# Turning the second product of pass B over to 512 columns of tokens, with block transposes on VectorE and stores in runs of 128 bytes

## The chip, the core and the metric

The kernel runs on one core of a Trainium2 chip. The metric is the device time of one execution in microseconds; 1086.42 us is the median of three runs before the change (1086.01 to 1088.9). TensorE (PE) multiplies, VectorE (DVE) and ScalarE (ACT) work elementwise, SyncE (SP) and GpSimd (POOL) start the DMAs. SBUF is the on-chip memory; PSUM holds TensorE's sums in eight banks, each of 128 partitions by 512 float32.

## The reference

Three stages, one after the other, all in float32, on 6016 tokens of 256 channels:

```
s = softmax over channels of (k normalised)^T (q normalised) / tau     # 256 x 256
x = v @ s                                                              # 6016 x 256
x = gelu(x @ moe_w_in) @ moe_w_out          # 256 -> 2048 -> 256   (pass A)
x = elu(x @ moe2_w_in) @ moe2_w_out         # 256 -> 2048 -> 256   (pass B)
```

gelu is h * sigmoid(1.702 h), elu is h for h > 0 and exp(h) - 1 otherwise. The softmax matrix is folded into moe_w_in, so that pass A starts from v.

## The kernel before

After a first phase that makes the 256 x 256 matrix, the kernel goes through two passes, A and B, of the same make. Each pass takes the tokens in six groups: five of 1024 tokens (8 slots of 128) and a last one of 896 (7 slots). Each group is computed in eight units p = 0 to 7, each for 256 of the 2048 hidden channels. A unit (kind, b, p) has two parts.

- The first product (`product`, L678) is a 2 x 2 block multiplication done with seven block products (the combinations of the operands are stored ahead), each of three matmuls of 512 columns, since every float32 operand is split into a high and a low part and high*high, high*low and low*high are summed. In the last group a matmul has 448 columns. The seven sums end in four quarters of the hidden values: C11, C12, C21 and C22 (hidden half i, token half X or Y).
- The nonlinearity takes each quarter through `s1` to `s4`: in pass B two ACT functions (L714, L715), two DVE operations (L725, L730), an ACT copy that is the high part (L737) and a DVE subtraction that is the low part (L741). L930 and L940 on DVE, L919 and L926 on ACT, make the sums that the block algorithm needs between its products.
- The second product (`second`) multiplies the hidden values by the second weight matrix and adds into PSUM banks 4 to 7 over all eight units of a group.

`step(t)` writes out the order by hand: it runs the first product and the nonlinearity of unit t, and between them, through `Q()`, the eight parts of the second product of unit t - 1. So TensorE's work in a step is product 1, Q, product 5, Q, products 6 and 2, two Qs, products 7 and 3, two Qs, product 4, two Qs. Every engine executes its instructions in the order in which they are written, and waits by semaphores. When unit t - 1 is the last of its group (p = 7), `step` calls `evacuate(before, 1)` after its sixth part (token half Y, banks 6 and 7), and `evacuate(before, 0)` early in the next step (token half X, banks 4 and 5). The next unit's second product, with p = 0, starts with half Y.

In pass A the second product is made with hidden channels in the rows of the stationary operand: a block of the weights (128 x 128) stays in TensorE and the hidden values of 512 tokens stream past it (L771), 24 matmuls per unit; the result has channels on the partitions and tokens along them. In pass B, 128 tokens of the hidden values are the stationary operand and 256 columns of weights stream past (L795), 48 matmuls per unit; the result has tokens on the partitions, as the output has. In pass B `evacuate` has four ACT copies per group from banks 4 to 7 to the tile `ob` (L825), and two DMAs on SP's queue, each partition writing four rows of the output, 4 KB in one run (L829).

During the first group of pass B, DVE and ACT also make the operands of the last group (`operands`, through `background(2)`, L964 in the listing: two pieces per step). At the end of each group SP's queue loads the seven operand tiles of the next one (L131).

Of the kernel before, what the change touches and what calls it, by code (L numbers as in the profile page):

```python
# [17 lines left out]
P = 128  # L18
# [4 lines left out]
def kernel(  # L23
# [40 lines left out]
    nc = tc.nc  # L64
    _, NT, C = q.shape
    DFF = w1.shape[1]
    KC = C // P
# [5 lines left out]
    HJ = SJ // 2  # L73
    groups = [(j, min(SJ, NJ - j)) for j in range(0, NJ, SJ)]
    NG = len(groups)
# [8 lines left out]
    ov = out.rearrange("(p j) c -> p j c", j=NJ)  # L84
# [13 lines left out]
    bank = [ps.tile([P, BANK], F32, name=f"b{i}") for i in range(8)]  # L98
# [290 lines left out]
    def full_tile(kind, b):  # L389
        full[kind, b] = stg.tile([P, KC, 2 * BANK], F32, tag="vt", name="vt")  # L390
        return full[kind, b]
# [111 lines left out]
    with tc.manual_schedule():  # L503
        make_identity(nc, ident)

        with ExitStack() as st:
# [24 lines left out]
            for i, m in enumerate(CHUNKS):  # L531
                t = wts.tile([P, 2, MM, C], F32, tag=f"wA{1 + i % 3}", name="qk")
# [6 lines left out]
                if i == 4:  # L539
                    nc.sync.dma_start(  # L540
                        out=tau_sb,
                        in_=tau.rearrange("(o a) -> o a", o=1).to_broadcast([P, 1]),
# [39 lines left out]
            for i in range(2):  # L582
                for c in range(KC):
                    x = i * KC + c
# [29 lines left out]
            e = ph1.tile([P, KC, C], F32, name="e")  # L614
            mn = ph1.tile([P, KC], F32, name="mn")
            sm = ph1.tile([P, KC], F32, name="sm")
            for c in range(KC):
                nc.vector.scalar_tensor_tensor(
                    out=e[:, c, :], in0=s_ps[c][:, :C], scalar=rk[:, c:c + 1], in1=rq,
# [125 lines left out]
        def fresh(key):  # L745

            if key in opened:
                return False
            opened.add(key)
            return True  # L750

        def acc_A(d, k):
            return 4 + 2 * k + d

        def second(u):

            kind, b, p = u
            n = wid[b]
            m = groups[b][1]
            w = w_second[kind, p]  # L760
            X, Y = 0, 1
            parts_ = []
            if kind == "A":
                seq = [(0, X), (0, Y), (1, Y), (1, X)] if p else [(0, Y), (0, X), (1, Y), (1, X)]
                for f, k in seq:
                    for d in range(KC):
                        def part(f=f, k=k, d=d):
                            g = g_t[kind, b, p, f]
                            a = acc_A(d, k)
                            for i, (wi, gi) in enumerate(((0, 0), (0, 1), (1, 0))):  # L770
                                nc.tensor.matmul(  # L771
                                    bank[a][:, :n],
                                    w[:, f, wi, d * P:(d + 1) * P],
                                    g[:, gi, k * n:(k + 1) * n],
                                    start=fresh((kind, b, a)),
                                    stop=(p == NP - 1 and f == 1 and i == 2),
                                    skip_group_check=True,
                                )
                        parts_.append(part)
            else:  # L780
                lowX = list(range(HJ)) if n == BANK else list(range(n // P))
                hiX = list(range(len(lowX), m))
                lowY = list(range(HJ, m))
                hiY = list(range(HJ))
                seq = [(0, lowX), (0, hiX), (1, lowY), (1, hiY)] if p else \
                    [(0, lowY), (0, hiY), (1, lowY), (1, hiY)]
                for f, slots in seq:
                    cut = (len(slots) + 1) // 2
                    for ss in (slots[:cut], slots[cut:]):
                        def part(f=f, ss=ss):  # L790
                            g = g_t[kind, b, p, f]
                            for s in ss:
                                a = 4 + s // 2
                                for gi, wi in ((0, 0), (0, 1), (1, 0)):
                                    nc.tensor.matmul(  # L795
                                        bank[a][:, s % 2 * C:(s % 2 + 1) * C],
                                        g[:, gi, s * P:(s + 1) * P],
                                        w[:, f, wi, :],
                                        start=fresh((kind, b, a)),
                                        stop=(p == NP - 1 and f == 1 and gi == 1),  # L800
                                        skip_group_check=True,
                                    )
                        parts_.append(part)
            return parts_
# [3 lines left out]
        def evacuate(u, k):  # L808

            kind, b, _ = u  # L810
            n = wid[b]
            j, m = groups[b]
            if kind == "A":
                t = full.get(("B", b))
                if t is None:
                    t = full_tile("B", b)
                for d in range(KC):
                    nc.scalar.copy(t[:, d, k * n:(k + 1) * n], bank[acc_A(d, k)][:, :n])
                return
            if b not in out_t:  # L820
                out_t[b] = tp.tile([P, SJ, C], F32, tag="ob", name="ob")
            o = out_t[b]
            for a in (0, 1) if k == 0 else (2, 3):
                w = min(2, m - 2 * a)
                nc.scalar.copy(  # L825
                    o[:, 2 * a:2 * a + w, :].rearrange("p s d -> p (s d)"), bank[4 + a][:, :w * C]
                )
            lo, hi = (0, HJ) if k == 0 else (HJ, m)
            nc.sync.dma_start(out=ov[:, j + lo:j + hi, :], in_=o[:, lo:hi, :])  # L829


# [24 lines left out]
        def step(t):  # L856
            nonlocal roles, late
            u = units[t] if t < len(units) else None
            before = units[t - 1] if t else None
            qs = second(before) if before else []  # L860
            last = before and before[2] == NP - 1

            def Q(n=1):
                for _ in range(n):
                    if not qs:
                        if not t:
                            spare(4)
                        return
                    qs.pop(0)()
                    if last and len(qs) == 2:  # L870
                        evacuate(before, 1)
                    if last and not qs:
                        if u is None:
                            evacuate(before, 0)
                        else:
                            late_out.append(lambda: evacuate(before, 0))
# [146 lines left out]
        for t in range(len(units) + 1):  # L1023
            u = units[t] if t < len(units) else None
            if u:
                kind, b, p = u
# [62 lines left out]
```

## Time and profile before

| | |
|---|---|
| median of three runs | 1086.42 us (1086.01 to 1088.9) |
| profiled execution | 1085.72 us, of which the span of the trace is 1084.0 us |
| granted TensorE clock, mean | 0.996 of full speed |
| TensorE matmul busy | 1056.2 us (97%), 5768 matmuls |
| VectorE busy | 830.6 us (77%) |
| ScalarE busy | 769.2 us (71%) |
| pass B, 40 slices view | TensorE 9 tenths or more, VectorE 8, DMA mostly 0 or 1 |

Busy TensorE time counts matmuls that overlap at their ends, so it says little of how much faster the work could go; what one step takes is read from the starts of successive matmuls in the timeline. The table's shares are means over a kernel with a first phase of some 65 us, a pass A and a pass B.

### The profile page before, as it was taken

What the parts mean: (1) busy time and instruction counts of PE and PEld (TensorE: products, weight loads), DVE (VectorE), ACT (ScalarE), POOL (GpSimd) and SP (SyncE); (2) the same over time, 40 slices, a digit from 0 to 9 for tenths busy, and PEclk for the clock granted to TensorE, in tenths of its full rate; (3) what the DMA queues carried; (4) which work ended last, traced back from release to release, by engine and by line L of the source; (5) the groups of instructions that cost most, each with busy time, mean ns of one, the idle gap of its engine ahead of it and who ended that gap; (6) DMA issues with size and microseconds to landing.
All of it is one profiled execution on the core that took longest, in us unless ns stands there. A gap on an engine that the chain in (4) does not pass through costs nothing.

```text
span 1084.0 us, 15552 instructions
## 1 busy us (share of the span) xinstructions
PE 1056.2 (97%) x5768; PEld 922.9 (85%) x5768; DVE 830.6 (77%) x1346; ACT 769.2 (71%) x1443; POOL 72.3 (7%) x126
## 2 busy tenths in 40 slices
PE   7978989999999999999899999999999999999998
PEld 6867868888888888888798998998998999999997
DVE  5888786677777776666437998888888888888886
ACT  5768767667767777676457777767677776767775
POOL 0000011012112221120000100000000000000000
PEclk9999999999999999999999999999999999999999
DMA  9913255358558557445745114004004003003100
GB/s 330 355 47 94 58 201 186 111 193 281 178 196 277 183 202 258 140 150 202 287 168 208 69 62 165 2 1 175 1 1 156 20 2 136 39 1 120 40 1 35
DMA packets 82845, 144.42 MB, mean 133 GB/s; under 512 B 46864, under 2 KB 51056, under 8 KB 82256
## 3 DMA queue, kind: packets, MB, share of 16 engines
q1 hardware_dynamic: 66624, 84.04, 23.2%
q0 software_dynamic: 16144, 59.38, 14.9%
q8 instruction: 45, 0.74, 0.3%
q14 instruction: 32, 0.26, 0.1%
HBM read 86.25 MB, written 57.15 MB: 132 GB/s over the span
## 4 chain that ended last, share of the span: by engine, by line
PE 63%; issue 15%; DVE 8%; ACT 6%; DMA 4%; POOL 3%; SPq 0%; POOLq 0%; DVEq 0%; ACTq 0%
PE b L678 29%; PE b L795 21%; PE b L771 11%; DMA qk<-in_k_dram 2%; DVE g L741 1%; DVE ee L725 1%; PE b L565 1%; DVE gg L730 1%; ACT ee L714 1%; ACT th L715 1%; DMA xdB<-xt 1%; POOL xdA L431 1%; POOL xdB L431 1%; PE b L474 1%; ACT g L737 1%
## 5 line engine op out<-in xcount | busy, mean ns | idle before, releaser
L795 PEld LDWEIGHTS b<-wBB,g 128*128 128x128 f32 x2256 | 301.7, 190 | 21.2 <-DVE g L741 2.3
L795 PE MATMUL b<-wBB,g 128*128 128x256 f32 x2256 | 309.0, 282 | 1.3 <-DVE g L741 1.0
L771 PE MATMUL b<-g,wBA 128*128 128x512 f32 (+1 forms) x1152 | 296.7, 386 | 1.7 <-DVE g L741 1.7
L678 PE MATMUL b<-xA,wAA 128*128 128x512 f32 (+1 forms) x1008 | 266.7, 388 | 9.7 <-ACT b L919 4.5
L678 PE MATMUL b<-xB,wAB 128*128 128x512 f32 (+1 forms) x1008 | 267.9, 389 | 0.2 <-DVE b L930 0.2
L771 PEld LDWEIGHTS b<-g,wBA 128*128 128x128 f32 x1152 | 216.9, 188 | 42.8 <-DVE g L741 2.2
L678 PEld LDWEIGHTS b<-xA,wAA 128*128 128x128 f32 x1008 | 188.0, 188 | 50.4 <-ACT b L919 8.4
L678 PEld LDWEIGHTS b<-xB,wAB 128*128 128x128 f32 x1008 | 174.2, 189 | 20.9 <-DVE b L930 0.4
L737 ACT CAST g<-gg 128x512 fp32r<-128x512 f32 (+1 forms) x192 | 118.3, 616 | 93.3 <-DVE gg L730 93.2
L725 DVE SCALAR_TENSOR_TENSOR ee<-ee,th 128x512 f32<-128x512 f32 (+1 forms) x192 | 129.9, 677 | 32.0 <-ACT th L715 31.9
L930 DVE TENSOR_TENSOR b<-b,s 128x512 f32<-128x512 f32 (+1 forms) x96 | 66.0, 687 | 111.7 <-PE b L678 105.3
L708 ACT ACTIVATE g<-b 128x512 fp32r<-128x512 f32 (+1 forms) x144 | 85.0, 590 | 86.8 <-PE b L678 86.3
L741 DVE TENSOR_TENSOR g<-gf,g 128x512 fp32r<-128x512 f32 (+1 forms) x192 | 128.4, 674 | 16.0 <-ACT gf L709 15.8
L741 DVE TENSOR_TENSOR g<-gg,g 128x512 fp32r<-128x512 f32 (+1 forms) x192 | 129.5, 675 | 11.0 <-ACT g L737 6.5
L714 ACT ACTIVATE ee<-b 128x512 f32<-128x512 f32 (+1 forms) x144 | 84.5, 587 | 34.8 <-PE b L678 34.6
L730 DVE SCALAR_TENSOR_TENSOR gg<-b,ee 128x512 f32<-128x512 f32 (+1 forms) x144 | 98.0, 680 | 4.9
L709 ACT ACTIVATE gf<-b 128x512 f32<-128x512 f32 (+1 forms) x144 | 84.4, 586 | 2.9 <-DVE g L741 2.5
L715 ACT ACTIVATE th<-b 128x512 f32<-128x512 f32 (+1 forms) x144 | 84.0, 583 | 0.0
L940 DVE TENSOR_TENSOR c<-b,s 128x512 f32<-128x512 f32 (+1 forms) x96 | 64.7, 674 | 23.1 <-PE b L678 22.9
L926 ACT COPY s<-b 128x512 f32<-128x512 f32 (+1 forms) x96 | 56.3, 586 | 27.0 <-PE b L678 26.1
L919 ACT COPY b<-b 128x512 f32<-128x512 f32 (+1 forms) x96 | 56.2, 585 | 16.9 <-PE b L678 16.8
L565 PE MATMUL b<-qk 128*128 128x256 f32 x188 | 44.1, 392 | 7.1 <-DMA qk<-in_k_dram 7.1
(98 smaller groups left out, 745.7 us busy)
## 6 DMA issues: line engine op xcount, KB each, us to landing
xdB<-xt POOLq DMA_DIRECT2D x35, 512.0 KB, 3.6
xB<-xdB SPq DMA_DIRECT2D x35, 512.0 KB, 5.3
xdA<-xt POOLq DMA_DIRECT2D x28, 512.0 KB, 3.2
xA<-xdA SPq DMA_DIRECT2D x28, 512.0 KB, 6.2
wAB<-w3d SPq DMA_DIRECT2D x4, 1792.0 KB, 7.9
out_dram<-ob SPq DMA_DIRECT2D x11, 512.0 KB, 2.6
qk<-in_q_dram SPq DMA_DIRECT2D x9, 512.0 KB, 6.4
qk<-in_k_dram SPq DMA_DIRECT2D x9, 512.0 KB, 7.3
```

Source lines behind the costliest of these rows:

```text
L678: nc.tensor.matmul(dst[:, :n], w[:, wi, p % 2, WOP[i], :], x[:, xi, :n], start=(start and k == 0), stop=(k == 2), skip_group_check=True,)
L708: nc.scalar.activation(self.sl(ik)[0], h, AF.Gelu_apprx_sigmoid)
L709: nc.scalar.activation(t[:, :n], h, AF.Gelu_apprx_sigmoid)
L714: nc.scalar.activation(e[:, :n], h, AF.Exp)
L715: nc.scalar.activation(t[:, :n], h, AF.Tanh, scale=0.5)
L725: nc.vector.scalar_tensor_tensor(out=e[:, :n], in0=e[:, :n], scalar=1.0, in1=t[:, :n], op0=ALU.add, op1=ALU.mult,)
L730: nc.vector.scalar_tensor_tensor(out=g[:, :n], in0=h, scalar=0.0, in1=e[:, :n], op0=ALU.max, op1=ALU.min)
L737: nc.scalar.copy(self.sl(ik)[0], self.tmp[ik][:, :self.n])
L741: nc.vector.tensor_sub(lo, self.tmp.pop(ik)[:, :self.n], hi.bitcast(F32))
L771: nc.tensor.matmul(bank[a][:, :n], w[:, f, wi, d * P:(d + 1) * P], g[:, gi, k * n:(k + 1) * n], start=fresh((kind, b, a)), stop=(p == NP - ...
L795: nc.tensor.matmul(bank[a][:, s % 2 * C:(s % 2 + 1) * C], g[:, gi, s * P:(s + 1) * P], w[:, f, wi, :], start=fresh((kind, b, a)), stop=(p ...
L930: nc.vector.tensor_add(bank[c][:, :n], bank[b][:, :n], s5[:, :n])
```

## The change

The second product of pass B takes the form that it has in pass A: the weights are the stationary operand and 512 columns of tokens stream past (in the changed kernel L776), 24 matmuls per unit in place of 48. This holds for the five groups of 1024 tokens; the last group keeps the rows (`by_rows`). The sums then lie with channels on the partitions. `evacuate` turns them on VectorE: per half of a group two transposes of 128 x 512 from PSUM to `ob` (L834), each of which transposes every square block of 32 x 32 by itself. The blocks are then not yet at their place across partitions, which the stores put right: 16 DMAs per half, each of 32 partitions with 8 runs of 32 floats, 128 bytes (L843). ScalarE's copies of these groups are gone.

```diff
+        def by_rows(kind, b):
+            return kind == "B" and b == NG - 1
...
-            if kind == "A":
+            if not by_rows(kind, b):
                 seq = [(0, X), (0, Y), (1, Y), (1, X)] if p else [(0, Y), (0, X), (1, Y), (1, X)]
...
+            lo, hi = (0, HJ) if k == 0 else (HJ, m)
+            if not by_rows(kind, b):
+                o = o.rearrange("p s (d x e) -> p s d x e", d=KC, e=32)
+                for d in range(KC):
+                    nc.vector.transpose(
+                        o[:, lo:hi, d, :, :].rearrange("p s x e -> p s (x e)"),
+                        bank[acc_A(d, k)][:, :n].rearrange("p (s t) -> p s t", t=P),
+                    )
+                dst = ov[:, j + lo:j + hi, :].rearrange(
+                    "(x p) s (d y e) -> x y p (s d) e", p=32, d=KC, e=32
+                )
+                for x in range(P // 32):
+                    for y in range(P // 32):
+                        nc.sync.dma_start(
+                            out=dst[x, y],
+                            in_=o[32 * y:32 * (y + 1), lo:hi, :, x, :].rearrange(
+                                "p s d e -> p (s d) e"
+                            ),
+                        )
+                return
             for a in (0, 1) if k == 0 else (2, 3):
```

On TensorE the order of the trains stays the same and each train of the second product changes its shape. The rows are the first products and parts of the step after the group change from the fourth to the fifth group of pass B (b_79 and the like are PSUM banks: 76 is bank 0, 80 to 83 are banks 4 to 7; xB and wAB belong to the first product). Before:

```order
L678 MATMUL b_79<-xB,wAB 128x512 x3
L795 MATMUL b_82<-wBB,g 128x256 x6
L678 MATMUL b_76<-xB,wAB 128x512 x3
L795 MATMUL b_83<-wBB,g 128x256 x6
L678 MATMUL b_78<-xB,wAB 128x512 x3
```

And in the changed kernel:

```order
L678 MATMUL b_79<-xB,wAB 128x512 x3
L776 MATMUL b_82<-g,wBB 128x512 x3
L678 MATMUL b_76<-xB,wAB 128x512 x3
L776 MATMUL b_83<-g,wBB 128x512 x3
L678 MATMUL b_78<-xB,wAB 128x512 x3
```

Nothing has moved against its neighbours; six matmuls of 256 columns have become three of 512.

On VectorE four transposes come into the order at each group change. The rows run from the low part of C11 in the first step of the fifth group to L930 of the next step (`ee`, `th`, `gg` are temporaries of the nonlinearity, `g` its result). Before:

```order
L741 TENSOR_TENSOR g<-gg,g 128x512
L725 SCALAR_TENSOR_TENSOR ee<-ee,th 128x512
L730 SCALAR_TENSOR_TENSOR gg<-b_78,ee 128x512
L741 TENSOR_TENSOR g<-gg,g 128x512
L725 SCALAR_TENSOR_TENSOR ee<-ee,th 128x512
L730 SCALAR_TENSOR_TENSOR gg<-c_8732,ee 128x512
L725 SCALAR_TENSOR_TENSOR ee<-ee,th 128x512
L730 SCALAR_TENSOR_TENSOR gg<-b_77,ee 128x512
L741 TENSOR_TENSOR g<-gg,g 128x512
L930 TENSOR_TENSOR b_77<-b_78,s_8848 128x512
```

And in the changed kernel, where L930 is L956:

```order
L834 STREAM_TRANSPOSE ob<-b_82 128x4x128
L834 STREAM_TRANSPOSE ob<-b_83 128x4x128
L725 SCALAR_TENSOR_TENSOR ee<-ee,th 128x512
L730 SCALAR_TENSOR_TENSOR gg<-b_78,ee 128x512
L741 TENSOR_TENSOR g<-gg,g 128x512
L725 SCALAR_TENSOR_TENSOR ee<-ee,th 128x512
L730 SCALAR_TENSOR_TENSOR gg<-c_8078,ee 128x512
L834 STREAM_TRANSPOSE ob<-b_80 128x4x128
L834 STREAM_TRANSPOSE ob<-b_81 128x4x128
L725 SCALAR_TENSOR_TENSOR ee<-ee,th 128x512
L730 SCALAR_TENSOR_TENSOR gg<-b_77,ee 128x512
L741 TENSOR_TENSOR g<-gg,g 128x512
```

The transposes of banks 6 and 7 stand behind the low part of C11 and ahead of the first operation on C12; those of banks 4 and 5 stand behind the operations on C22 and ahead of those on C21. The rest keeps its order. On SP's queue the 32 stores of a group stand where its two stores stood: behind the operand loads of the next group and ahead of those of the one after that.

## Rows read from the trace of the kernel before

**Rows 1.** The page's first part: busy time and share of each engine.
```profile
PE 1056.2 (97%) x5768; PEld 922.9 (85%) x5768; DVE 830.6 (77%) x1346; ACT 769.2 (71%) x1443; POOL 72.3 (7%) x126
```
**Rows 2.** Timeline, TensorE, pass A: start, duration (us), engine, line, operation, count.
```profile
381.30 0.84 PE L678 MATMUL b<-xA,wAA 128*128 128x512 f32 x3
...
384.02 1.52 PE L678 MATMUL b<-xA,wAA 128*128 128x512 f32 x6
385.38 1.52 PE L771 MATMUL b<-g,wBA 128*128 128x512 f32 x6
...
391.50 0.84 PE L678 MATMUL b<-xA,wAA 128*128 128x512 f32 x3
```
**Rows 3.** Timeline, TensorE, within a step of pass B.
```profile
703.48 1.55 PE L678 MATMUL b<-xB,wAB 128*128 128x512 f32 x6
...
704.87 1.60 PE L795 MATMUL b<-wBB,g 128*128 128x256 f32 x12
...
706.30 1.55 PE L678 MATMUL b<-xB,wAB 128*128 128x512 f32 x6
```
**Rows 4.** Timeline, a group change of pass B; brackets: idle before, releaser.
```profile
742.99 0.86 PE L678 MATMUL b<-xB,wAB 128*128 128x512 f32 x3
...
746.75 0.70 DVE L930 TENSOR_TENSOR b<-b,s 128x512 f32<-128x512 f32 x1 [0.46 <-PE b L678]
...
747.19 1.60 PE L795 MATMUL b<-wBB,g 128*128 128x256 f32 x12
...
748.51 0.69 DVE L725 SCALAR_TENSOR_TENSOR ee<-ee,th 128x512 f32<-128x512 f32 x1 [0.47 <-ACT th L715]
...
749.24 0.69 DVE L730 SCALAR_TENSOR_TENSOR gg<-b,ee 128x512 f32<-128x512 f32 x1
...
750.62 0.69 DVE L741 TENSOR_TENSOR g<-gg,g 128x512 fp32r<-128x512 f32 x1
...
751.46 1.08 ACT L825 COPY ob<-b 128x512 f32<-128x512 f32 x2
751.60 0.69 DVE L725 SCALAR_TENSOR_TENSOR ee<-ee,th 128x512 f32<-128x512 f32 x1 [0.29 <-ACT th L715]
...
753.57 0.86 PE L678 MATMUL b<-xB,wAB 128*128 128x512 f32 x3
...
754.12 0.69 DVE L741 TENSOR_TENSOR g<-gg,g 128x512 fp32r<-128x512 f32 x1 [1.10 <-ACT g L737]
...
754.73 0.69 DVE L725 SCALAR_TENSOR_TENSOR ee<-ee,th 128x512 f32<-128x512 f32 x1
...
754.87 0.74 PE L795 MATMUL b<-wBB,g 128*128 128x256 f32 x4 [0.21 <-DVE g L741]
...
755.45 0.69 DVE L730 SCALAR_TENSOR_TENSOR gg<-c,ee 128x512 f32<-128x512 f32 x1
```
**Rows 5.** The same view where TensorE's next but one step starts.
```profile
764.62 0.86 PE L678 MATMUL b<-xB,wAB 128*128 128x512 f32 x3
```
**Rows 6.** Chain of waits in the first group of pass B: start, duration, what.
```profile
587.67 0.60 ACT ee L714
588.27 0.50 ACT th L715
...
631.66 1.65 PE b L678 x6
```
**Rows 7.** VectorE by line and form: count, busy us, mean ns, idle before.
```profile
L930 DVE TENSOR_TENSOR b<-b,s 128x512 f32<-128x512 f32 x80 | 55.9, 698 | 87.0 <-PE b L678 82.5 <-ACT xt L425 3.4 <-ACT wBA L245 1.0
L207 DVE TENSOR_SCALAR bits<-raw 128x512 int32<-128x512 int32 x32 | 14.2, 444 | 0.0
L378 DVE STREAM_TRANSPOSE vt<-v_raw 128x512 f32<-128x512 f32 x18 | 12.5, 702 | 10.8 <-DMA v_raw<-in_v_dram 10.8
L523 DVE TENSOR_TENSOR sq<-sq 128x1024 f32<-128x1024 f32 x9 | 11.0, 1224 | 6.8 <-ACT sq L549 6.8
```
**Rows 8.** Timeline, SyncE's queue in pass A: one half of a group of v.
```profile
202.71 8.46 SPq L371 DMA_DIRECT2D v_raw<-in_v_dram  x16
```

More of the change, by code (lines that the diff above doesn't have):

```diff
@@ L827, in evacuate @@
                 )
-            lo, hi = (0, HJ) if k == 0 else (HJ, m)
             nc.sync.dma_start(out=ov[:, j + lo:j + hi, :], in_=o[:, lo:hi, :])
```

## The prediction, made before the changed kernel ran

> **What bounds the kernel now.** I read the page's busy shares first: TensorE is busy for 97% of the span, VectorE for 77%, ScalarE for 71% [rows 1]. Busy time of overlapping matmuls says little about what a cheaper form would give, so the timelines of the two passes come next, read by starts. In pass A six matmuls of 512 columns take 385.38 - 384.02 = 1.36 us, whichever product they belong to, and a whole step of 15 trains of three lasts 391.50 - 381.30 = 10.20 us, which is 15 x 0.68 [rows 2]. In pass B six of 512 take 704.87 - 703.48 = 1.39 us, the twelve of 256 that stand in for six of 512 take 706.30 - 704.87 = 1.43 us [rows 3], and a whole step lasts 753.57 - 742.99 = 10.58 us [rows 4]. So in both passes TensorE sets the pace of an ordinary step, and the same column count costs 0.38 us more in the row form of B: 8 trains at 0.035 us more, the rest in the first products between them.
>
> VectorE is the engine next to the bound. In an ordinary step of B it stands still three times, 0.46 us for TensorE, 0.47 us for ScalarE behind TensorE, and 0.29 us for ScalarE behind VectorE itself [rows 4]. The last of these goes round within VectorE and ScalarE and does not shrink with TensorE; so VectorE's own round is about 10.58 - 0.46 - 0.47 = 9.65 us, still under 10.20.
>
> There are two kinds of place where that reserve is not there. One is the first group of B, in which the operands of the last group are made beside the steps: there the chain of waits, from 587.67 us until TensorE's product at 631.66 us, runs through ScalarE and VectorE with no TensorE piece in it [rows 6]. The other is the step after each group change: it lasts 764.62 - 753.57 = 11.05 us, 0.47 us too long [rows 4, 5], since TensorE waits for the low part of C12, which VectorE makes at 754.12 us behind ScalarE's two copies to `ob`.
>
> **The change, part by part.**
>
> *The matmuls.* Forty second products are turned over (five groups of eight units). The order of trains is then that of pass A, with the same shapes and the same sizes of operands; I take pass A's 10.20 us per step. 40 x 0.38 = 15.2 us off TensorE's path (the last of them runs beside products of 448 columns and is counted like the others). From below, the gain is nothing, if the spacing stays at 10.58; from above I see no row under 10.20.
>
> *The first group.* Of these 15.2 us, those between 587.67 and 631.66 us do not come: the chain there does not touch TensorE, and its VectorE and ScalarE work is unchanged. That stretch is four steps and a train pair, of which TensorE would save 4 x 0.38 + 0.07 = 1.6 us. The wait for VectorE at its end grows by that. 15.2 - 1.6 = 13.6.
>
> *The transposes.* Per group four of 128 x 512, from PSUM, on VectorE; they replace four copies on ScalarE, where time is not short. The trace has no block transpose from PSUM. The nearest rows: a transpose of the same size from SBUF takes 0.702 us, an addition that reads PSUM takes 0.698 us [rows 7]. I take 0.70. Bounds: from below the fastest operation on 512 elements, 0.444 us; from above one over 1024 elements, 1.224 us, which would be the price if a transpose from PSUM went at half rate [rows 7].
>
> [...]
>
> What queues behind them: VectorE executes in order, so the first pair (banks 6 and 7) delays C12, the second pair (banks 4 and 5) delays C21 and L930. I go through one group change with zero at product 1 of its first step, TensorE at 0.68 us a train. VectorE's L725 for C11 comes at 748.51 - 742.99 = 5.52 us before; it hangs on product 2, which ends at 6 x 0.68 = 4.08 instead of 747.19 - 742.99 = 4.20, so 5.40. L741 for C11 follows 750.62 - 748.51 = 2.11 later: 7.51. One operation comes 0.61 after an independent one (754.73 - 754.12), and 0.72 after one whose result it reads (755.45 - 754.73) [rows 4]. First transpose 8.12, second 8.75 (its bank is finished at 12 x 0.68 = 8.16 and a little), L725 for C12 at 9.38, L730 at 10.10, L741 1.38 later (750.62 - 749.24) at 11.48, finished at 12.17, at TensorE some 0.06 later (754.87 - 754.12 - 0.69). TensorE wants it with the second matmul of the next step's first part, at 10.20 + 0.68 + 0.23 = 11.11. It waits 1.12 us.
>
> Going on: L725 for C22 12.09, L730 12.81, transposes 13.42 and 14.05, L725 for C21 14.68, L730 15.40, L741 16.01, L930 16.61 to 17.31. Product 7 overwrites what L930 reads; TensorE wants to start it at 10.20 + 8 x 0.68 + 1.12 = 16.76 and gets it at 17.35: another 0.59 us. Nothing later is short: banks 4 and 5 are free at 14.75, wanted at 15.4, and VectorE gains about 0.55 us on TensorE per step from here. So each change costs 1.71 us in place of 0.47, 1.24 more; five of them 6.2 us.
>
> *ScalarE.* Four copies per group go. They hide in no bound except at the change, where the copies made L737 late; there VectorE's queue is later still, so their going gives nothing more.
>
> *The stores.* Per group 32 DMAs in place of 2, all on SP's queue. Sixteen loads of the same cut (32 partitions, 128-byte runs) hold SP for 8.46 us [rows 8], so the stores hold it for some 17 us. Behind them stand the operand loads of the group after, six to seven steps or over 60 us later; `ob` is next written after 80 us; the last group, whose stores end the kernel, is not changed. I count nothing. The cover would be gone only if 32 stores took over four times as long as 32 loads.
>
> [...] No row of before shows such a store; the loads of the same cut are in rows 8.
>
> *Sum.* 15.2 - 1.6 - 6.2 = 7.4 us less. The profiled execution of 1085.72 us would be 1078.3; it lies 0.7 us under the median, so the median goes from 1086.42 to 1079.0 us, 0.7% faster.
>
> **The rivals.**
>
> *A. The group change costs no more than before.* VectorE's three stops per step hold 1.22 us, and if the transposes fell into them, only the first group would be lost: 1086.42 - 13.6 = 1072.8 us. Against it: the transposes must wait for the sums in banks 6 and 7, and by then VectorE's next operand is almost there.
>
> *B. A transpose from PSUM is slow, and the result is slower than before.* All four of a change stand in VectorE's order ahead of L930, so each tenth of a microsecond more costs 0.4 us per change and 2.0 us in all. At 1.224 us: 20 x 0.52 = 10.4 us more, 1089.4 us. It decides from 0.70 + 7.4 / 20 = 1.07 us per transpose on. For it: a transpose turns 32 columns into 32 partitions, and none from PSUM was seen. Against it: neither transposes nor operands in PSUM are dear in rows 7. At 0.444 us it would go the other way, to 1073.9.
>
> *C. No gain per step.* Either three matmuls of 512 do not go at 0.68 us here, or VectorE's round is really above 10.20 us and becomes the bound; then steps stay at 10.58. The change at that pace: C12's low part at 12.35 us against 11.52 wanted, then L930 late by 0.43 more, 1.26 us against 0.47; five times 0.8 is 4 us lost: 1090.4 us. For it: VectorE's margin per step is only 0.55 us. Against it: pass A runs the same trains, and two of the three stops are for TensorE.
>
> *D. The stores hold up the loads.* If 32 stores took five times 17 us, 85 us, the next group's operands would come some 15 us late or more, four times: about 1140 us. Nothing in the trace speaks for it but the missing row.
>
> **How the numbers follow.** Forecast 0.67, A 0.11, B 0.10, C 0.09, D 0.03. The forecast's own range is 1076 to 1083 (0.16 us either way on a transpose is 3 us, and 0.3 us on a change 1.5 us). The range of 1072 to 1086 leaves out the slow end of B, C and D, and a little of A. A measurement of this kernel can tell a difference of about 0.3%, 3.3 us; faster means under 1083.2. The forecast is that for nearly all of its chance, A for all, B for its fast end: 0.79. B between 0.9 and 1.2 us a transpose, and a forecast that lost a few more microseconds, fall within: 0.08. The rest of B, C and D: 0.13.
>
> **What would show it.** Starts of products in an ordinary step of B 10.20 us apart from the second group on, and no shorter in the first group between its second and fifth step. L834 at about 0.70 us. The step after a change near 11.9 us, with TensorE waiting once for L741 and once for L956. SP finished with the 32 stores long before the next operand loads. The prediction is wrong if steps stay above 10.3 us, if L834 takes over 0.9 us, or if a change costs under 0.8 us or over 2.5 us.

## The result and the profile after

The changed kernel takes 1078.53 us (median of four runs, 1078.05 to 1079.06) against 1086.32 for the kernel before in the same comparison, a ratio of 0.9919 with a 95% interval of 0.9905 to 0.9933: 7.8 us, 0.8% less. The prediction said 1079.0 us. The profiled execution took 1078.05 us, with a span of 1076.3 us.

The page's first part of the changed kernel answers [rows 1]:

```profile
PE 1047.0 (97%) x4808; PEld 873.5 (81%) x4808; DVE 840.7 (78%) x1366; ACT 759.6 (71%) x1423; POOL 72.1 (7%) x126
```

TensorE has 960 matmuls fewer, VectorE 20 operations more, ScalarE 20 fewer, and the shares are as good as unchanged: from this line nobody could tell that the kernel is faster. The steps tell it. The timeline of the changed kernel around the group change that [rows 4, 5] show for before:

```profile
740.00 0.84 PE L678 MATMUL b<-xB,wAB 128*128 128x512 f32 x3
...
744.08 1.52 PE L776 MATMUL b<-g,wBB 128*128 128x512 f32 x6
...
745.44 1.52 PE L678 MATMUL b<-xB,wAB 128*128 128x512 f32 x6
...
747.50 0.69 DVE L741 TENSOR_TENSOR g<-gg,g 128x512 fp32r<-128x512 f32 x1
...
748.11 1.31 DVE L834 STREAM_TRANSPOSE ob<-b 128x512 f32<-128x512 f32 x2
...
749.34 0.65 DVE L725 SCALAR_TENSOR_TENSOR ee<-ee,th 128x512 f32<-128x512 f32 x1
749.45 16.39 SPq L843 DMA_DIRECT2D out_dram<-ob  x32
...
750.20 0.84 PE L678 MATMUL b<-xB,wAB 128*128 128x512 f32 x3
...
751.40 0.69 DVE L741 TENSOR_TENSOR g<-gg,g 128x512 fp32r<-128x512 f32 x1 [0.68 <-ACT g L737]
751.43 0.49 PE L776 MATMUL b<-g,wBB 128*128 128x512 f32 x1 [0.39 <-ACT g L737]
...
752.15 0.74 PE L776 MATMUL b<-g,wBB 128*128 128x512 f32 x2 [0.23 <-DVE g L741]
...
752.73 0.87 PE L678 MATMUL b<-xB,wAB 128*128 128x512 f32 x3
...
753.34 1.31 DVE L834 STREAM_TRANSPOSE ob<-b 128x512 f32<-128x512 f32 x2
...
756.47 0.69 DVE L956 TENSOR_TENSOR b<-b,s 128x512 f32<-128x512 f32 x1
...
757.21 1.65 PE L678 MATMUL b<-xB,wAB 128*128 128x512 f32 x6 [0.19 <-DVE b L956]
...
758.71 1.52 PE L776 MATMUL b<-g,wBB 128*128 128x512 f32 x6
...
762.11 0.84 PE L678 MATMUL b<-xB,wAB 128*128 128x512 f32 x3
```

Read it by starts. An ordinary step lasts 750.20 - 740.00 = 10.20 us, where it was 10.58; six matmuls of the second product take 745.44 - 744.08 = 1.36 us, where twelve narrow ones took 1.43 [rows 3]. The step after the change lasts 762.11 - 750.20 = 11.91 us, where it was 11.05 [rows 4, 5]. In it TensorE waits where its three brackets stand. Two of them are at the first part of the second product: it waits for the high part of C12 (L737, at 751.43), and one matmul later for the low part (L741, at 752.15). The third is for L956, before product 7. In front of the first two stands the first pair of L834 on VectorE, in front of the third both pairs. L741 of C11 (747.50) and L956 (756.47) keep their places around them; the listing of the changed kernel's order ahead begins behind the one and ends in front of the other.

The first group of B gained nothing from the start of step 2 to that of step 6 (steps are counted from 0). Before:

```profile
593.86 0.86 PE L678 MATMUL b<-xB,wAB 128*128 128x512 f32 x3
...
631.66 1.65 PE L678 MATMUL b<-xB,wAB 128*128 128x512 f32 x6 [0.23 <-DVE b L930]
...
636.72 0.86 PE L678 MATMUL b<-xB,wAB 128*128 128x512 f32 x3
```

And in the changed kernel:

```profile
593.31 0.84 PE L678 MATMUL b<-xB,wAB 128*128 128x512 f32 x3
...
620.23 1.66 PE L678 MATMUL b<-xB,wAB 128*128 128x512 f32 x6 [0.34 <-DVE b L956]
...
631.30 1.65 PE L678 MATMUL b<-xB,wAB 128*128 128x512 f32 x6 [0.44 <-DVE b L956]
...
636.19 0.84 PE L678 MATMUL b<-xB,wAB 128*128 128x512 f32 x3
```

These four steps last 42.86 us before and 42.88 after; what TensorE would have saved it now waits for VectorE, at 620.23 and at 631.30, where before only the second wait was there, and shorter.

For all that the change touches, take pass B from product 1 of its step 1 to that of its last step: 1064.27 - 582.25 = 482.02 us before and 1056.88 - 582.00 = 474.88 after, 7.14 us less. The granted clock was 1.00 in both stretches, so the difference is not the clock's. This measure is better than the whole time for what follows, since the part ahead of pass B, the same in all kernels here, ended between 582.0 and 586.8 us in the profiled executions.

### The profile page after: what moved, and what is told of

Same layout as the page of the kernel before. It is cut to its first block, busy times and chain, and to the rows that moved or that the text cites. A ratio compares the mean times of both kernels' runs of the same rounds, so it can differ in the third digit from the quotient of the medians.

```text
span 1076.3 us, 13797 instructions
## 1 busy us (share of the span) xinstructions
PE 1047.0 (97%) x4808; PEld 873.5 (81%) x4808; DVE 840.7 (78%) x1366; ACT 759.6 (71%) x1423; POOL 72.1 (7%) x126
## 4 chain that ended last, share of the span: by engine, by line
PE 61%; issue 16%; DVE 12%; ACT 5%; POOL 3%; DMA 3%; SPq 0%; DVEq 0%; POOLq 0%; ACTq 0%
PE b L678 28%; PE b L776 28%; PE b L800 4%; DVE gg L730 2%; DVE ee L725 2%; DVE sq L523 1%; DVE g L741 1%; DMA qk<-in_k_dram 1%; DVE ob L834 1%; DMA xdB<-xt 1%; PE b L474 1%; POOL xdA L431 1%; ACT g L737 1%; POOL xdB L431 1%; DVE b L956 1%
## 5 line engine op out<-in xcount | busy, mean ns | idle before, releaser
L776 PE MATMUL b<-g,wBA 128*128 128x512 f32 (+1 forms) x1152 | 296.6, 386 | 1.7 <-DVE g L741 1.7
L776 PE MATMUL b<-g,wBB 128*128 128x512 f32 x960 | 252.3, 390 | 2.9 <-ACT g L737 1.8
L776 PEld LDWEIGHTS b<-g,wBA 128*128 128x128 f32 x1152 | 216.9, 188 | 42.9 <-DVE g L741 2.2
L678 PEld LDWEIGHTS b<-xB,wAB 128*128 128x128 f32 x1008 | 186.3, 188 | 40.0 <-DVE b L956 4.6
L776 PEld LDWEIGHTS b<-g,wBB 128*128 128x128 f32 x960 | 179.8, 188 | 43.4 <-ACT g L737 3.9
L737 ACT CAST g<-gg 128x512 fp32r<-128x512 f32 (+1 forms) x192 | 117.9, 614 | 114.2 <-DVE gg L730 110.1
L956 DVE TENSOR_TENSOR b<-b,s 128x512 f32<-128x512 f32 (+1 forms) x96 | 65.9, 687 | 100.9 <-PE b L678 93.5
L741 DVE TENSOR_TENSOR g<-gf,g 128x512 fp32r<-128x512 f32 (+1 forms) x192 | 128.5, 674 | 16.0 <-ACT gf L709 15.8
L741 DVE TENSOR_TENSOR g<-gg,g 128x512 fp32r<-128x512 f32 (+1 forms) x192 | 129.4, 674 | 8.9 <-ACT g L737 4.4
```

What stands on the lines that cost most here:

```text
L678: nc.tensor.matmul(dst[:, :n], w[:, wi, p % 2, WOP[i], :], x[:, xi, :n], start=(start and k == 0), stop=(k == 2), skip_group_check=True,)
L737: nc.scalar.copy(self.sl(ik)[0], self.tmp[ik][:, :self.n])
L741: nc.vector.tensor_sub(lo, self.tmp.pop(ik)[:, :self.n], hi.bitcast(F32))
L776: nc.tensor.matmul(bank[a][:, :n], w[:, f, wi, d * P:(d + 1) * P], g[:, gi, k * n:(k + 1) * n], start=fresh((kind, b, a)), stop=(p == NP - ...
L956: nc.vector.tensor_add(bank[c][:, :n], bank[b][:, :n], s5[:, :n])
```

## The experiments

The theory: the gain is the step of 10.20 us in place of 10.58, and the price is VectorE's order at the group change and in the first group. The rivals: the price comes from the quicker matmuls or the first use of C12 by themselves; the gain comes in part from ScalarE's freed copies; the stores disturb something.

**The transposes taken away (e1_act_copy).**

```diff
-                    nc.vector.transpose(
+                    nc.scalar.copy(
                         o[:, lo:hi, d, :, :].rearrange("p s x e -> p s (x e)"),
```

> The changed kernel with the 20 block transposes on VectorE replaced by 20 plain copies on ScalarE at the same places in the program; the blocks stay unturned, so the layout of the output is left out. Theory (VectorE's order at the group change sets its price): the first pair of copies starts at 8.36 us of the step, when the bank is finished, puts L737 of C12 at 10.35 and L741 at 11.0 to 11.7, so TensorE waits 0.66 us at each change in place of 1.71; 5 x 1.05 = 5.2 us less than the changed kernel, 1073.3 us. Rival 1 (the wait at the change comes from the quicker matmuls alone, or from the new p = 0 order, not from the transposes): no change, 1078.5. Rival 2 (ScalarE's freed time was part of the gain): slower than the changed kernel, 1080 or more.

Measured 1075.37 us (1073.5 to 1076.28), ratio to before 0.9897 (0.9880 to 0.9914). Expected were 1073.3 us. In the trace pass B takes 470.13 us, 4.75 less than in the changed kernel, where 5.2 were expected. Timeline around the same change:

```profile
751.81 0.84 PE L678 MATMUL b<-xB,wAB 128*128 128x512 f32 x3
...
752.62 0.69 DVE L741 TENSOR_TENSOR g<-gg,g 128x512 fp32r<-128x512 f32 x1 [1.10 <-ACT g L737]
...
753.36 0.73 PE L776 MATMUL b<-g,wBB 128*128 128x512 f32 x2 [0.23 <-DVE g L741]
...
762.79 0.84 PE L678 MATMUL b<-xB,wAB 128*128 128x512 f32 x3
```

The step lasts 10.98 us, the wait for L956 is gone, and 0.78 us of the first wait is left (0.66 expected). So 0.93 us of the 1.71 per change is the transposes' place in VectorE's order; the rest is there with copies too, as 0.47 us of it was before. Rival 2 is refuted: with twenty more copies on ScalarE than the changed kernel has, the kernel is quicker. Rival 1 is refuted for the larger part; for the other 0.78 us this run leaves it open, since the copies stand in the way of C12 as well (e7_deferred_only below divides it).

**Each transpose twice (e3_twice).**

```diff
                 for d in range(KC):
-                    nc.vector.transpose(
...
+                    for _ in range(2):
+                        nc.vector.transpose(
...
```

> The changed kernel with every block transpose done twice in a row. Theory: four more operations of 0.62 us in VectorE's order per change; C12's low part comes 1.24 us later, L956 2.48 us later, so TensorE waits 4.19 us per change in place of 1.71; 5 x 2.48 = 12.4 us, 1090.9 us, slower than the kernel before the change. Rival (the transposes fall into VectorE's stops and the change's price is something else): under 3 us more, below 1081.5.

Measured 1093.98 us (1092.73 to 1094.88), ratio 1.0067 (1.0048 to 1.0086); pass B takes 491.27 us, 16.4 more than in the changed kernel, where 12.4 were expected.

```profile
751.52 2.81 DVE L835 STREAM_TRANSPOSE ob<-b 128x512 f32<-128x512 f32 x4
...
753.61 0.84 PE L678 MATMUL b<-xB,wAB 128*128 128x512 f32 x3
...
756.33 0.50 PE L776 MATMUL b<-g,wBB 128*128 128x512 f32 x1 [1.88 <-ACT g L737]
...
763.61 1.64 PE L678 MATMUL b<-xB,wAB 128*128 128x512 f32 x6 [1.54 <-DVE b L957]
...
768.49 0.84 PE L678 MATMUL b<-xB,wAB 128*128 128x512 f32 x3
```

The step after the change lasts 14.88 us, 2.97 more than 11.91, and the others of that size 2.95 to 3.00 more. The mechanism is right, each added transpose goes straight to TensorE's waits, but its price was too low: four of them take 2.81 us here and a pair 1.31, so a set of four adds 1.50 us and not 1.24, which with two sets per change is about the missing 0.49. Part of this is the repetition itself. In the set shown the transposes start at 751.52, 752.26, 752.90 and 753.61: a repeat, which writes the same place once more, comes 0.74 or 0.71 us after the first, a transpose of the other bank 0.64 us.

The last change, beside products of 448 columns, lasts 15.12 us where it was 10.62, so it costs 4.50 us more, 1.53 beyond the 2.97 of the others. That is not the transposes' own time: TensorE's granted clock fell there. TensorE's rows, and the sums of two stretches, the one ahead of the fall and the one in it (busy us of PE, PEld, DVE, ACT and POOL, then the granted clock, DMA share and GB/s):

```profile
1021.23 2.14 PE L678 MATMUL b<-xB,wAB 128*128 128x448 f32 x6 [1.27 <-DVE b L957]
...
1025.09 0.83 PE L678 MATMUL b<-xB,wAB 128*128 128x448 f32 x3
```

```profile
1012.00:1021.20 9.20, 5.97 (x35) 4.79 (x33) 8.40 (x15) 3.94 (x9) 0.00 (x0) 1.00 0.39 57
1022.00:1025.00 3.00, 3.00 (x13) 2.83 (x13) 2.60 (x5) 2.07 (x5) 0.00 (x0) 0.50 0.45 66
```

And the same trains in the changed kernel:

```profile
1005.92 1.50 PE L678 MATMUL b<-xB,wAB 128*128 128x448 f32 x6 [0.29 <-DVE b L956]
...
1008.33 0.77 PE L678 MATMUL b<-xB,wAB 128*128 128x448 f32 x3
```

From 1012.00 to 1021.20 us TensorE was busy for 5.97 of 9.20 us at a clock of 1.00, in the last of its waits it stood still for 1.27 us, and from 1022 to 1025 us it was granted a clock of 0.50. The trains from product 7 to product 4 took 1025.09 - 1021.23 = 3.86 us where they take 1008.33 - 1005.92 = 2.41 at a clock of 1.00: 1.45 of the 1.53 us. Three of the other four changes hold trains as slow (three matmuls of 512 columns in 1.48 us at 671.77 and at 930.66, six in 2.29 us at 846.11, where the run's usual trains take 0.84 and 1.52) and last 14.90 or 14.91 us, against 14.88 in the one without. There the slow trains stand between the first wait and the one for L957, which was shorter by about as much (0.16 us at 936.20 where it is 1.54 above), so the steps do not show it.

**The evacuation alone (e5_rows_turned).**

```diff
-            if not by_rows(kind, b):
+            if kind == "A":
                 seq = [(0, X), (0, Y), (1, Y), (1, X)] if p else [(0, Y), (0, X), (1, Y), (1, X)]
```

> The evacuation part of the change alone: the second product of pass B keeps the row form of the kernel before in all groups, and VectorE turns its sums and the 128-byte stores carry them out; the layout of the output is left out. Theory (the gain is the matmul form, the transposes only cost): steps stay at 10.58 us, a change costs 1.26 us in place of 0.47, 5 x 0.8 = 4.0 us more than the kernel before, 1090.4 us. Rival (ScalarE's freed copies or the other stores are where the gain is from): 1083 us or less.

Measured 1091.48 us (1089.77 to 1092.68), ratio 1.0045 (1.0030 to 1.0060). Pass B takes 486.05 us, 4.03 more than before; expected were 4.0.

```profile
754.70 0.86 PE L678 MATMUL b<-xB,wAB 128*128 128x512 f32 x3
...
756.39 0.74 PE L800 MATMUL b<-wBB,g 128*128 128x256 f32 x4 [0.23 <-DVE g L741]
...
757.58 1.31 DVE L834 STREAM_TRANSPOSE ob<-b 128x512 f32<-128x512 f32 x2
...
761.45 1.66 PE L678 MATMUL b<-xB,wAB 128*128 128x512 f32 x6
...
766.50 0.86 PE L678 MATMUL b<-xB,wAB 128*128 128x512 f32 x3
```

The step after a change lasts 11.80 us where it was 11.05, ordinary steps stay at 10.58. So the transposes and stores only cost, and all of the gain is the matmul form: 4.03 + 7.14 = 11.2 us of it, net of its own longer waits.

**The old stores (e2_two_stores).**

```diff
-                dst = ov[:, j + lo:j + hi, :].rearrange(
...
+                nc.sync.dma_start(
+                    out=ov[:, j + lo:j + hi, :].rearrange("p s c -> p (s c)"),
+                    in_=o[:, lo:hi, :, :, :].rearrange("p s d x e -> p (s d x e)"),
                 )
-                for x in range(P // 32):
-                    for y in range(P // 32):
-                        nc.sync.dma_start(
-                            out=dst[x, y],
...
```

> The changed kernel with the old stores: two DMAs per group with runs of 4 KB, so that blocks land at the wrong place in the output. Theory: nobody waits for the stores, 1078.5 us within 1. Rival (32 stores of 128-byte runs disturb the other transfers or SP's queue): 1 to 4 us less.

Measured 1079.95 us (1078.67 to 1083.01), ratio 0.9945 (0.9929 to 0.9960); pass B takes 474.75 us against 474.88. The stores in short runs cost nothing there. The median came out 0.5 us above the range that was expected (1078.5 within 1); in the trace, which is of the execution of 1083.01 us, what differs is the part ahead of pass B, which ends 4.8 us later. The DMA queues in 22 us around a change show what is hidden. First with the old stores, then in the changed kernel (queue, packets, MB, share of 16 engines):

```profile
q1 hardware_dynamic: 288, 1.05, 11.9%
```

```profile
q1 hardware_dynamic: 8704, 1.05, 32.9%
```

The same 1.05 MB take 2.8 times the DMA engines' time, in a stretch in which the profile shows no other DMA of the kernel.

**The operands of the last group spread thinner (e4_spread).**

```diff
             if not A:
-                background(2)
+                if u[1] == 0:
+                    background(2 if u[2] == 1 else 1)
+                elif u[2] == 2:
+                    background(2)
```

> The changed kernel with the making of the last group's operands spread thinner in the first group of pass B: two pieces in step 1, one in each of steps 2 to 7, the last two in step 2 of the second group, where it was two per step in steps 1 to 5. Theory (the first group gains nothing because VectorE's chain sets its pace there): the first group's steps 2 to 6, 53.2 us in the changed kernel, go to about 51.2, 1.5 to 2.0 us less in the whole, 1076.8 us; the other steps as before. Rival (the first group is slow for another reason, the loads of weights or operands): no change, 1078.5.

Measured 1078.06 us (1075.94 to 1079.83), ratio 0.9912 (0.9894 to 0.9929); by the whole time not to be told from the changed kernel. In the trace steps 2 to 6 of the first group take 51.36 us (53.18 in the changed kernel, 51.2 expected):

```profile
596.66 0.84 PE L678 MATMUL b<-xB,wAB 128*128 128x512 f32 x3
...
648.02 0.84 PE L678 MATMUL b<-xB,wAB 128*128 128x512 f32 x3
```

The first change is 0.28 us longer, since VectorE comes to it late, and pass B takes 473.28 us, 1.60 less. The rival of slow loads is refuted: no load was moved.

**Copies by ScalarE, transposes one per step (e6_deferred, e7_deferred_only).** The core of the edit:

```diff
+        def copy_out(b, k, d):
+            if (b, k) not in sums:
+                sums[b, k] = stage([P, KC, BANK], "sm").bitcast(F32)
+            nc.scalar.copy(sums[b, k][:, d, :], bank[acc_A(d, k)])
+            turns.append((b, k, d))
...
             tail(1)
             U.s1(C11)
+            if not A and u[2] >= 2:
+                turn()
...
             U.s1(C22)
+            if split:
+                copy_out(before[1], 1, 0)
...
             U.s1(C21)
+            if split:
+                copy_out(before[1], 1, 1)
```

`turn` is one transpose from SBUF, and after the second of a half the sixteen stores. Banks 4 and 5 are copied where their evacuation stood. e6_deferred has the thinner spread of e4_spread beside this, e7_deferred_only has not.

> A version meant to beat both: ScalarE copies the four banks of a group to SBUF in gaps of its own (bank 6 behind the functions of C22, bank 7 behind those of C21, banks 4 and 5 behind L945 of the next step), VectorE turns one block row per step in steps 2 to 5 of the next group, where it has 0.55 us of reserve each; operands of the last group spread thinner as in the run with that alone. Theory: at a change only C12's low part is 0.23 us late, so the step after a change takes 10.4 to 10.5 us in place of 11.91; 5 x 1.45 = 7.3 us, with 1.7 of the first group 9.0 us less than the changed kernel, 1069.5 us. Rival 1 (the change's price is the first use of C12 in the p = 0 order and not VectorE's queue): over 11 us for that step, 1074 or more. Rival 2 (VectorE's reserve per step is not there): steps 2 to 5 of a group longer by 0.2 to 0.6 us each, 4 to 12 us given back.

> The same deferral without the thinner spread of the operands. Theory: the step after a change as with both, 10.4 to 10.5 us, the first group as in the changed kernel; 1071.2 us. If the two parts hang together (a late first group that spoils the first change), the first change alone is longer.

Both parts: 1071.24 us (1069.63 to 1072.04), ratio 0.9848 (0.9830 to 0.9867) against the changed kernel's 0.9919. Deferral only: 1072.97 us (1072.41 to 1074.07), ratio 0.9868 (0.9847 to 0.9889). Pass B takes 466.71 and 468.16 us, 8.17 and 6.72 less than in the changed kernel (9.0 and 7.3 expected). A change and one of the later steps of e6_deferred:

```profile
748.40 0.59 ACT L818 COPY sm<-b 128x512 f32<-128x512 f32 x1
749.21 0.84 PE L678 MATMUL b<-xB,wAB 128*128 128x512 f32 x3
749.61 0.69 DVE L741 TENSOR_TENSOR g<-gg,g 128x512 fp32r<-128x512 f32 x1 [0.69 <-ACT g L737]
...
750.44 0.59 ACT L818 COPY sm<-b 128x512 f32<-128x512 f32 x1
...
759.82 0.84 PE L678 MATMUL b<-xB,wAB 128*128 128x512 f32 x3
```

```profile
770.02 0.84 PE L678 MATMUL b<-xB,wAB 128*128 128x512 f32 x3
...
774.88 0.70 DVE L830 STREAM_TRANSPOSE ob<-sm 128x512 f32<-128x512 f32 x1
...
778.55 0.69 DVE L725 SCALAR_TENSOR_TENSOR ee<-ee,th 128x512 f32<-128x512 f32 x1 [0.29 <-ACT th L715]
...
780.22 0.84 PE L678 MATMUL b<-xB,wAB 128*128 128x512 f32 x3
```

The step after this change takes 10.61 us (10.4 to 10.5 expected), and the steps that hold a transpose stay at 10.20: the same VectorE work costs nothing where a step has reserve for it. Both rivals are refuted. Of the 0.78 us that e1_act_copy left, 0.37 to 0.41 is still there in the full-size changes of both runs (but for the first of e6_deferred), where no transpose stands ahead of C12's operations and no copy holds them up; the quicker matmuls and the first use of C12 can be the cause of no more than that, and which of them it is stays open. With both parts the first change is 10.94 us, with deferral only 10.57: the thinner spread lets VectorE come late to the first change, which eats 0.37 of its 1.8 us.

## Why the prediction was right, by its own steps

- *The matmuls.* Right: 10.20 us per ordinary step, the number taken from pass A. Step 40, beside products of 448 columns, went from 10.00 to 9.78 us and not by the 0.38 it was counted with.
- *The first group.* Right: 42.86 us before, 42.88 after, and the run with the spread gives 1.60 us of pass B back. The chain was not quite as foretold: in the changed kernel the first two of the four steps still gain 0.18 us, and the other two give it back.
- *The transposes.* 0.691 us each from PSUM against 0.70 taken; no row of before had such a transpose, and from SBUF one took 0.702 us [rows 7]. That refutes rival B. Two in a pair start 0.63 us apart.
- *The order at the change.* 11.91 us foretold, 11.91, 11.91, 11.95 and 11.93 measured in the full-size changes. In detail the first wait was a little longer and in two pieces, for L737 and then for L741, where one was foretold (product 5 at 752.73 where 750.20 + 1.36 = 751.56 is its place: 1.17 us, 1.12 foretold), and the second was 0.35 us (757.21 against 755.50 + 1.36) and not 0.59. What made up for it was not in the sum: the six matmuls after that wait took 758.71 - 757.21 = 1.50 us and not 1.36. So the waits are where the prediction has them, and that the step agrees to the hundredth is in part luck. The last change cost 1.16 us more than before, 1.24 foretold.
- *ScalarE and the stores.* Nothing counted, nothing found: e1_act_copy and e2_two_stores. SP was held for 15.6 to 17.0 us per group, 17 foretold. The runs of 128 bytes took 32.9% of the DMA engines' time and the runs of 4 KB 11.9%, for the same bytes, and it decides nothing here, since nobody waits.
- *The sum.* 7.4 us foretold, 7.14 in pass B. The remaining 0.6 us of the difference of the medians lies within what the part ahead of pass B scatters, and I ascribe it to nothing; that the median came within 0.5 us of the forecast is luck to that extent.

Rival A is refuted by the changes of 11.91 us, rival D by e2_two_stores. Rival C's price, 4 us for the evacuation at the old pace, was confirmed by e5_rows_turned, though the rival itself did not come about. The terms that came out were those read as distances between starts in undisturbed steps, and the one in-order queue gone through operation by operation.

## What to carry to other kernels

Price a matmul form by the starts of successive trains where the same form already runs in the kernel; busy time and matmul counts do not give it (TensorE was busy for 97% before and after, with 960 matmuls fewer). Work that was moved to an engine with a reserve per step was free here only where it was spread over the steps as the reserve is: the same four transposes cost 1.3 us per change in two pairs (11.91 against 10.57 us, with the copies placed in gaps) and nothing one per step. Where the chain of waits has no piece of the engine that is made faster, count no gain there (42.86 us before, 42.88 after in the first group). And look at the granted clock before a cost in one place is put down to an edit: in e3_twice, where it fell to 0.50, that was 1.45 us of one step.

## What the runs showed of the hardware that was not expected

- After a wait TensorE's next six matmuls took 1.50 us from start to start of the following train (757.21 to 758.71), where six later in the same step took 1.36 (758.71 to 760.07); in e3_twice they took 1.48 (763.61 to 765.09). The granted clock was 1.00 in both. So these two waits, of 0.19 and 1.54 us in their brackets, came with 0.14 and 0.12 us more.
- A block transpose that repeats the one before it, from the same bank to the same place, started 0.71 to 0.74 us after it (e3_twice), one from the other bank 0.63 to 0.64 us.
- In e3_twice the granted clock was 0.50 from 1022 to 1025 us, in the last of the five group changes, in which TensorE had stood still for 1.56 us and then for 1.27. Three other changes, each with a wait of 1.88 us, had trains as slow (1.48 us where 0.84 is usual, 2.29 where 1.52 is); the one around 753.61, with the same wait of 1.88 us, had none, and its clock was 1.00. In pass B of the changed kernel, with waits of 0.2 to 0.4 us, it stayed at 1.00.
- Stores in runs of 128 bytes landed 1.6 us after issue (median, 32 KB each) and held SP for 15.6 to 17.0 us per group, about 0.5 us each, against 8.46 us for 16 loads of the same cut [rows 8].
